# Two kept K/V units, small output-weight loads and new weight layouts in a two-layer decode kernel

## The chip, the cores and the metric

The kernel runs on one core of a Trainium2 chip. The metric is the device time of one execution in microseconds (us). Before the change the median of three runs was 2663.63 us (2663.0 to 2664.99).

Names used below: PE is the tensor engine, DVE the vector engine, ACT the scalar engine, POOL the GpSimd engine, SP the sync engine, which issues nearly all DMAs here. A "unit" is one (batch, head) pair; there are 64 units in a layer. A "tile" is half of a unit's K or V, 2 MB. "Slot" is a place of 16 KB per partition in the ring buffer in SBUF.

## The reference, cut to what matters

```python
B, Sq, D = 2, 1, 576
H, Sk, Dh = 32, 16384, 128        # k_cache, v_cache: (B, H, Sk, Dh) bf16, 268 MB each
F = 4608

def _A_ref(x, k_cache, v_cache, wq, wo):
    q = (x @ wq).reshape(B, Sq, H, Dh).transpose(0, 2, 1, 3)
    p = softmax(einsum("bhqd,bhkd->bhqk", q, k_cache) * Dh ** -0.5)
    o = einsum("bhqk,bhkd->bhqd", p, v_cache)
    return o.transpose(0, 2, 1, 3).reshape(B, Sq, H * Dh) @ wo

def _B_ref(x, w1, w2, w3, w4):     # S = 1: the shifted mixer is zero, hs = 0 @ w2
    x1 = x + hs
    return x1 + gelu(layernorm(x1) @ w3) @ w4

for layer in range(2):             # the same caches and weights in both layers
    x = x + _A_ref(layernorm(x), k_cache, v_cache, wq, wo)
    x = x + _B_ref(layernorm(x), w1, w2, w3, w4)
```

Both layers read the whole K and V caches. One query row per unit is used, so each byte that is read is used once per layer: the kernel is a stream of K and V through SBUF.

## The kernel before

Everything large passes through one ring of 12 slots. Tiles are wanted in the order of `plan`, and `pump` issues the next DMA as soon as the place that the ring points to is free. A place is the next address, with kept tiles stepped over.

```python
class Ring:
    def _place(self, n, aligned):
        p = self.at
        ...
        for _ in range(4 * len(self.live) + 4):
            if p + n > self.size:
                p = 0
            kept = [t for t in self.live if t["keep"] and t["off"] < p + n and p < t["off"] + t["n"]]
            if not kept:
                return p
            p = max(t["off"] + t["n"] for t in kept)
            ...

    def pump(self):
        while self.queue:
            key, n, src, aligned = self.queue[0]
            p = self._place(n, aligned)
            ...
            under = [t for t in self.live if t["off"] < p + n and p < t["off"] + t["n"]]
            if not all(t["done"] for t in under):
                return                                   # the next address is still in use: wait
            ...                                          # else issue the DMA into it
```

The order of the loads: the second layer walks the units backwards, so the last unit of layer 1 can be kept. The output weights wo come as eight blocks of 1152 KB in the same queue, one at every 16th unit, just before V.

```python
    GH = 8                 # heads in one output sum
    N_KEEP = 1             # units kept from layer 1
        self.order = [list(range(self.U)), list(reversed(range(self.U)))]
        kept = self.order[0][-self.N_KEEP:] if self.N_KEEP else []
        ...
            for i, u in enumerate(order):
                if u not in skip:
                    for h in range(2):
                        ring.want(("K", l, u, h), TB * 128, kv(self.K, u, h))
                ...
                if i >= 1:
                    self.want_v(kv, l, i - 1, skip, jrows)
            self.want_v(kv, l, self.U - 1, skip, jrows)
            for k in range(self.KT):
                ring.want(("w3", l, k), self.F, krows(self.w3, k, 0, self.F), aligned=(k == 0))
            for j in range(0, self.MT, 12):
                ring.want(("w4", l, j // 12), 12 * D, jrows(self.w4, j, 12), aligned=False)
            if l == 0:
                want_wq(1)

    def want_v(self, kv, l, i, skip, jrows):
        u = self.order[l][i]
        if (i + 1) % (self.GH * self.B) == 0:
            h0 = self.group_base(l, i)
            self.ring.want(("wo", l, h0), self.GH * self.D, jrows(self.wo, h0, self.GH))
        ...
```

w4 and wo are read in rows of 576 elements, 1152 bytes. PE has two jobs on a unit: it transposes half of K's blocks and multiplies them by the query, and it "weighs" V by the softmax weights with 128 matmuls.

```python
        def f(pe):                                        # weigh: one half of V
            for j in range(self.TB):
                ins = pe.matmul(self.ops[g][:, col:col + 1], lhsT=vt[:, j * 128:(j + 1) * 128],
                                rhs=self.p[q][:, h * self.TB + j:h * self.TB + j + 1], ...)
```

## Time and profile before

| | before |
|---|---|
| median of 3 runs | 2663.63 us |
| span of the profiled run | 2663.4 us |
| read from HBM | 1106.13 MB |
| busy: DVE, PE, ACT | 74%, 59%, 41% |
| K and V loads in the chain that ended last | 63% of the span |

These lines are from the page of the kernel before: the span; the busy tenths of the DMA engines and the rate in GB/s, each in 40 equal slices of 66.6 us; and the DMA queues with packets, megabytes and share of the 16 engines.

```profile
span 2663.4 us, 74240 instructions
...
DMA  9999999999999999999999999999999999999998
GB/s 393 426 426 427 424 419 426 426 426 408 426 426 426 426 407 426 426 426 425 357 401 421 426 426 422 426 427 425 426 392 426 426 427 426 407 426 426 427 426 300
...
q1 hardware_dynamic: 94072, 1106.16, 99.0%
q8 instruction: 270, 4.42, 0.7%
...
HBM read 1106.13 MB, written 0.00 MB: 415 GB/s over the span
```

The rate stands at 426 GB/s in most slices. It dips to 392 to 408 in four slices (wo blocks), to 357 at the layer boundary, and to 300 at the end.

The windows view gives the same for chosen stretches (length, busy time and number of instructions per engine, granted clock, mean busy share of the 16 DMA engines, GB/s): the layer boundary, one wo block, and the end.

```profile
core 0: us, PE busy (x) PEld busy (x) DVE busy (x) ACT busy (x) POOL busy (x), PEclk, DMA share, GB/s
1312.00:1360.00 48.00, 22.74 (x597) 21.48 (x598) 7.17 (x32) 3.71 (x11) 0.00 (x0) 0.50 1.02 328
1968.00:1978.00 10.00, 7.04 (x124) 6.79 (x125) 5.80 (x10) 3.90 (x5) 0.00 (x0) 0.51 0.63 247
2612.00:2664.00 52.00, 21.59 (x609) 19.88 (x609) 11.03 (x35) 2.22 (x10) 0.00 (x0) 0.50 0.84 289
```

At the wo block the DMA share falls to 0.63 and the rate to 247 GB/s. At the boundary the engines are busy (1.02) at a low rate: the packets there are small.

The timeline of the issuing queue around the start of layer 2 (start, length, engine, line, what is loaded, how many DMAs):

```profile
start us, us, engine line op out<-in xcount [idle before <-releaser]
...
1354.59 2.83 SPq L296 DMA_DIRECT2D ring<-in_A_k_cache_dram  x2
1379.17 9.31 SPq L296 DMA_DIRECT2D ring<-in_A_v_cache_dram  x2
1395.82 0.33 SPq L296 DMA_DIRECT2D ring<-in_A_k_cache_dram  x1
```

Between these issues the queue has enough tiles in hand. The slices here stay above 400 GB/s.

### The profile page before, as it was taken

What the parts mean: (1) busy time and instruction counts of PE and PEld (TensorE: products, weight loads), DVE (VectorE), ACT (ScalarE), POOL (GpSimd) and SP (SyncE); (2) the same over time, 40 slices, a digit from 0 to 9 for tenths busy, and PEclk for the clock granted to TensorE, in tenths of its full rate; (3) what the DMA queues carried; (4) which work ended last, traced back from release to release, by engine and by line L of the source; (5) the groups of instructions that cost most, each with busy time, mean ns of one, the idle gap of its engine ahead of it and who ended that gap; (6) DMA issues with size and microseconds to landing.
All of it is one profiled execution on the core that took longest, in us unless ns stands there. A gap on an engine that the chain in (4) does not pass through costs nothing.

```text
span 2663.4 us, 74240 instructions
## 1 busy us (share of the span) xinstructions
PE 1558.8 (59%) x34587; PEld 1461.0 (55%) x34587; DVE 1979.6 (74%) x2649; ACT 1098.5 (41%) x1681; POOL 0.8 (0%) x10
## 2 busy tenths in 40 slices
PE   4665565555556555556467565665556556556654
PEld 4555555555555555555457555555555555555554
DVE  5877877777777777787559777777777777777773
ACT  3444344344334434434235344344334434434431
POOL 0000000000000000000000000000000000000000
PEclk8666666666666666666566666666666666666665
DMA  9999999999999999999999999999999999999998
GB/s 393 426 426 427 424 419 426 426 426 408 426 426 426 426 407 426 426 426 425 357 401 421 426 426 422 426 427 425 426 392 426 426 427 426 407 426 426 427 426 300
DMA packets 94380, 1110.90 MB, mean 417 GB/s; under 512 B 8756, under 2 KB 26744, under 8 KB 26744
## 3 DMA queue, kind: packets, MB, share of 16 engines
q1 hardware_dynamic: 94072, 1106.16, 99.0%
q8 instruction: 270, 4.42, 0.7%
q14 instruction: 38, 0.31, 0.0%
HBM read 1106.13 MB, written 0.00 MB: 415 GB/s over the span
## 4 chain that ended last, share of the span: by engine, by line
DMA 67%; PE 11%; DVE 8%; another core or an unknown queue 8%; ACT 4%; SPq 1%; issue 1%
DMA ring<-in_A_v_cache_dram 35%; DMA ring<-in_A_k_cache_dram 28%; DVE sd L572 5%; PE ops L617 5%; PE tps L539 4%; DMA ring<-in_B_w_dram 4%; ACT ktsb L543 3%; DVE prod L569 3%; PE sps L557 1%; PE misc L590 1%; DMA ring<-in_A_wq_dram 1%; ACT p L603 1%; SPq L301 0%; PE misc L457 0%
## 5 line engine op out<-in xcount | busy, mean ns | idle before, releaser
L572 DVE TENSOR_REDUCE sd<-prod 128x8 f32<-128x1024 bf16 x1024 | 1249.0, 1220 | 35.4
L543 ACT ACTIVATE ktsb<-tps 128x1024 bf16<-128x1024 bf16 x1024 | 992.7, 1028 | 514.6 <-PE tps L539 509.1
L539 PE MATMUL tps<-ident,ring 128*128 128x128 bf16 x8192 | 829.2, 268 | 336.8 <-DMA ring<-in_A_k_cache_dram 336.8
L569 DVE TENSOR_TENSOR prod<-ring,qb 128x1024 bf16<-128x1024 bf16 x1024 | 698.7, 682 | 256.0 <-DMA ring<-in_A_k_cache_dram 255.3
L539 PEld LDWEIGHTS tps<-ident,ring 128*128 128x128 bf16 x8192 | 673.4, 123 | 366.5 <-DMA ring<-in_A_k_cache_dram 358.6
L617 PE MATMUL ops<-p,ring 128*128 128x1 bf16 x16384 | 471.2, 165 | 564.8 <-DMA ring<-in_A_v_cache_dram 555.2
L617 PEld LDWEIGHTS ops<-p,ring 128*128 128x128 bf16 x16384 | 450.1, 102 | 585.8 <-DMA ring<-in_A_v_cache_dram 571.7
L526 ACT ACTIVATE qb<-misc 128x128 bf16<-128x128 f32 x128 | 35.5, 277 | 941.8 <-PE misc L524 941.8
L557 PE MATMUL sps<-qt,ktsb 128*128 128x1 bf16 x8192 | 349.9, 166 | 93.4 <-ACT ktsb L543 85.1
L557 PEld LDWEIGHTS sps<-qt,ktsb 128*128 128x128 bf16 x8192 | 313.0, 102 | 132.8 <-ACT ktsb L543 131.6
L592 DVE TENSOR_REDUCE bias<-misc 128x1 f32<-128x128 f32 x128 | 37.3, 291 | 260.6 <-PE misc L590 260.6
L590 PE MATMUL misc<-identS,m 128*128 128x128 f32 x256 | 95.5, 476 | 34.6 <-DVE m L584 34.6
L590 PEld LDWEIGHTS misc<-identS,m 128*128 128x128 f32 x256 | 69.7, 333 | 37.2 <-DVE m L584 37.1
L603 ACT ACTIVATE p<-sps,bias 128x64 bf16<-128x64 f32 x128 | 40.5, 317 | 23.8 <-DVE bias L592 23.8
L603 ACT ACTIVATE p<-sd,bias 128x64 bf16<-128x64 f32 x128 | 45.4, 354 | 0.0
L448 PE MATMUL sps<-xn,ring 128*128 128x2 bf16 (+1 forms) x680 | 20.6, 165 | 30.0 <-DMA ring<-in_A_wq_dram 15.6
L448 PEld LDWEIGHTS sps<-xn,ring 128*128 128x128 bf16 (+1 forms) x680 | 19.4, 104 | 31.2 <-DMA ring<-in_A_wq_dram 13.8
L524 PE MATMUL misc<-ident,qt 128*128 128x128 bf16 x128 | 34.3, 268 | 2.2 <-DVE xa L649 1.6
L580 DVE TENSOR_REDUCE m<-sps 128x1 f32<-128x64 f32 x128 | 27.4, 214 | 0.0
L603 ACT ACTIVATION_READ_ACCUMULATOR p<-sps,bias 128x1 f32 x128 | 27.1, 212 | 0.0
L582 DVE TENSOR_REDUCE m<-sd 128x1 f32<-128x64 f32 x128 | 26.6, 208 | 0.0
L603 ACT ACTIVATION_READ_ACCUMULATOR p<-sd,bias 128x1 f32 x128 | 26.5, 207 | 0.0
(63 smaller groups left out, 123.4 us busy)
## 6 DMA issues: line engine op xcount, KB each, us to landing
ring<-in_A_k_cache_dram SPq DMA_DIRECT2D x254, 2048.0 KB, 46.5
ring<-in_A_v_cache_dram SPq DMA_DIRECT2D x254, 2048.0 KB, 50.4
ring<-in_B_w_dram SPq DMA_DIRECT2D x6, 1728.0 KB, 35.5
ring<-in_A_wo_dram SPq DMA_DIRECT2D x8, 1152.0 KB, 48.7
ring<-in_B_w_dram SPq DMA_DIRECT2D x8, 1152.0 KB, 23.4
ring<-in_A_wq_dram SPq DMA_DIRECT2D x8, 1024.0 KB, 10.6
ring<-in_B_w_dram SPq DMA_DIRECT2D x2, 576.0 KB, 31.9
ring<-in_A_wq_dram SPq DMA_DIRECT2D x2, 512.0 KB, 16.6
```

What stands on the lines that cost most here:

```text
L448: ins = pe.matmul(out[:, m * self.B:(m + 1) * self.B], lhsT=w[lo:128, m * 128:(m + 1) * 128], rhs=self.xn[lo:128, k, :], start=(k == 0 and ...
L524: self.pe(lambda pe: pe.matmul(self.misc[:, 0:128], lhsT=bcast(self.qt[:, u:u + 1], 128), rhs=self.ident[:, :], start=True, stop=True), r= ...
L526: self.act(lambda a: a.activation(out=self.qb[q][:, :], in_=self.misc[:, 0:128], func=ACT.Copy), r=["P:misc"], w=[f"qb{q}"])
L539: ins = pe.transpose(self.tps[b][:, j * 128:(j + 1) * 128], kt[:, (j0 + j) * 128:(j0 + j + 1) * 128], self.ident[:, :])
L543: self.act(lambda a: a.activation(out=self.ktsb[k][:, :, :].rearrange("p a b -> p (a b)"), in_=self.tps[b][:, :], func=ACT.Copy), r=[f"P:t ...
L557: ins = pe.matmul(self.sps[sp][:, col:col + 1], lhsT=self.ktsb[k][:, j, :], rhs=self.qt[:, u:u + 1], start=True, stop=True)
L569: self.dve(lambda v: v.tensor_tensor(out=self.prod[d][:, :, :], in0=k3, in1=bcast_mid(self.qb[q][:, :], self.CH), op=ALU.mult), r=[res, f" ...
L572: self.dve(lambda v: v.tensor_reduce(out=self.sd[q][:, o:o + self.CH], in_=self.prod[d][:, :, :], axis=AX.X, op=ALU.add), r=[f"prod{d}"], ...
L590: self.pe(lambda pe: pe.matmul(self.misc[:, 128:256], lhsT=bcast(self.m[:, q:q + 1], 128), rhs=self.identS[:, :], start=True, stop=True), ...
L592: self.dve(lambda v: v.tensor_reduce(out=self.bias[:, q:q + 1], in_=self.misc[:, 128:256], axis=AX.X, op=ALU.max, negate=True), r=["P:misc ...
L603: self.act(lambda a, c0=c0, c1=c1, src=src, part=part: a.activation(out=self.p[q][:, c0:c1], in_=src, func=ACT.Exp, bias=self.bias[:, q:q ...
L617: ins = pe.matmul(self.ops[g][:, col:col + 1], lhsT=vt[:, j * 128:(j + 1) * 128], rhs=self.p[q][:, h * self.TB + j:h * self.TB + j + 1], s ...
```

## The change

The intent is to read 8.4 MB less and to lose less DMA time. It keeps two units (eight tiles) instead of one for layer 2; takes wo out of the ring and loads it as 32 pieces of 288 KB on ACT's queue; lays w4 out in rows of 4608 bytes (four rows of the matrix per partition) with smaller last pieces; loads the last 64 rows of w3 and wq as two halves into both partition halves; and loads w2 as one tile, later. The core of the diff, with cuts:

```diff
-    GH = 8
-    N_KEEP = 1
+    GH = 2
+    N_KEEP = 2
+    FJ = 4
+    W4_PIECES = (3, 3, 2, 1)
...
+        self.wobuf = sb("wobuf", [128, self.GH, self.D], BF16)
...
-            ap = w[k * 128:D, c0:c1]
-            return lambda e, v: e.dma_start(v[self.p0:128, :], ap)
+            a0, a1 = w[k * 128:D, 0:cut], w[k * 128:D, n - cut:n]
+            return cut, [lambda e, v: e.dma_start(v[0:64, 0:cut], a0),
+                         lambda e, v: e.dma_start(v[64:128, 0:cut], a1)]
...
+        def frows(a0, n):
+            ap = self.w4[a0 * 128 * self.FJ:(a0 + n) * 128 * self.FJ, :].rearrange(
+                "(a p j) n -> p a (j n)", p=128, j=self.FJ)
+            return [lambda e, v: e.dma_start(v.rearrange("p (a m) -> p a m", a=n), ap)]
...
-            for j in range(0, self.MT, 12):
-                ring.want(("w4", l, j // 12), 12 * D, jrows(self.w4, j, 12), aligned=False)
+            a0 = 0
+            for c, n in enumerate(self.W4_PIECES):
+                ring.want(("w4", l, c), n * self.FJ * D, frows(a0, n), aligned=False)
+                a0 += n
...
-        if (i + 1) % (self.GH * self.B) == 0:
-            h0 = self.group_base(l, i)
-            self.ring.want(("wo", l, h0), self.GH * self.D, jrows(self.wo, h0, self.GH))
...
+    def load_wo(self, l, i):
+        h0 = self.group_base(l, i)
+        ap = self.wo[h0 * 128:(h0 + self.GH) * 128, :].rearrange("(j p) n -> p j n", p=128)
+        self.s.dma(lambda e: e.dma_start(self.wobuf[:, :, :], ap), w=["wobuf"], eng="scalar")
...
+                if i % n == 1 and c == 6:
+                    self.load_wo(l, i)
```

The ring's rule of placing (next address, kept tiles stepped over, wait if the tile there is in use) is not touched.

## The prediction

> **What bounds the kernel.** HBM reads. The DMA row of the slices is 9 nearly everywhere at 425 to 428 GB/s, and two thirds of the chain that ended last are K and V loads; DVE is busy 74%, PE 59%. The kernel moves 1110.9 MB (DMA line). At 426.5 GB/s that is 2605 us; some 59 us are DMA time lost. By windows: about 22 us around the eight 1.15 MB wo loads (1152 B rows; 247 GB/s in 1968 to 1978), about 11 us at the layer boundary (328 GB/s in 1312 to 1360), about 15 us after the last V tile (289 GB/s in 2612 to 2664), about 6 us at the start.
>
> **What the change does.**
> 1. Four more K/V tiles (8.39 MB) are not read again: -19.7 us of DMA time; doubled w3 columns cost +0.3.
> 2. wo comes as 32 small loads on the ACT queue instead of blocks inside the K/V queue. They keep 1152 B rows (0.051 us a packet; at the rate of 16 KB rows 0.043), so about 4 of the 22 us stay: -18 us.
> 3. w4 in rows of 4.6 KB and more: most of the loss at the boundary and the end, -5 to -6 us at each, including a last piece of 20 matmuls (about 0.6 us) instead of 60 (1.76 us).
> 4. The last rows of w3 and wq go to both partition halves, each by its own DMA. The Trainium skill, "SBUF — State Buffer", section '"Can I just issue two DMAs to hit both halves?"', says that such DMAs serialize. Before, single 64-partition loads coincide with stretches of 203 to 264 GB/s (windows), which agrees with half rate for one; no run shows two yet. I count no gain.
> 5. group_out runs 32 times instead of 8. No cost: DVE needs 15.5 us a unit where DMA needs 19.7.
>
> **The new wait.** Two kept units hold 8 of the 12 ring slots. Through four slots pass w3, w4, the next wq, then K of the third and fourth unit of layer 2. The ring places in address order, and the slot after these tiles holds K of the third unit, first half. So the next V load waits until layer 2 has gone through both kept units and that half, although kept slots come free before. In the trace of before that half is released 38.4 us after the layer's first query row (1357.4 to 1395.8, where a DMA issue ends its wait); this pace is DVE's, so it stays. The four tiles queued behind wq last only 4 x 4.9 = 19.7 us, and landing signal and issue add 2 to 4 us. I expect one DMA hole of about 22 us some 20 us into layer 2, which eats all of step 1. After it DMA bounds again.
>
> **Sum.** 2663 - 19.7 + 0.3 - 18 - 11.5 + 22 = 2636; I say 2634 us, range 2616 to 2648. All lies on the critical path, the DMA queue.
>
> Chances: faster by over 2%: 0.08; within 2%: 0.91; slower: 0.01.
>
> **What would show it.** Step 1: HBM read about 1097.9 MB. New wait: about 20 us with DMA share near 0 some 60 us after the last V tile of layer 1, the issuing queue waiting for a K transpose. Step 2: no dips below 415 GB/s every 16 units. Step 3: from the last V tile's weighing to the end about 32 us instead of 37.7.
>
> **What would make it wrong.** If the ring reuses freed kept slots in time, the time falls to about 2614. If small wo packets slow both queues, or ACT is held at issue, up to 10 us come back. If the two half loads run beside each other, 3 to 5 us less.

## The result, and the profile after

| | before | after |
|---|---|---|
| median | 2663.97 us (4 runs, 2663.0 to 2664.99) | 2664.78 us (4 runs, 2662.82 to 2666.54) |
| ratio, 95% interval | | 1.0003 (0.9985 to 1.002) |
| span of the profiled run | 2663.4 us | 2660.8 us |
| read from HBM | 1106.13 MB | 1097.87 MB |

A ratio here and below is the mean time of one kernel's fast runs over the mean of the other's fast runs of the same rounds, so it is not quite the ratio of the medians that are quoted. The change makes no difference that these runs can show. The prediction was 2634 us with a range up to 2648: a fall of some 30 us that did not come. The result lies 17 us above the range. The chance of 0.91 for "within 2%" was well placed, but only because the predicted fall was itself under 2%.

The page of the kernel after, the same lines as of before, with the new queue of the wo loads (q10) and PE's count of instructions:

```profile
span 2660.8 us, 74381 instructions
...
PE 1570.0 (59%) x34580; PEld 1474.1 (55%) x34580; DVE 1994.1 (75%) x2753; ACT 1098.3 (41%) x1681; POOL 0.9 (0%) x11
...
DMA  9999999999999999999869999999999999999997
GB/s 388 425 426 426 425 424 426 426 426 425 425 425 426 425 425 425 425 425 425 338 249 425 424 427 424 426 425 425 425 426 425 426 425 425 427 425 425 425 425 293
...
q1 hardware_dynamic: 78072, 1088.47, 97.0%
q10 hardware_dynamic: 8704, 9.44, 1.0%
q8 instruction: 270, 4.42, 0.7%
...
HBM read 1097.87 MB, written 0.00 MB: 413 GB/s over the span
```

The wo dips are gone: slices 10, 15, 30 and 35 stand at 425 to 427. The bytes fell as intended. But a slice of 249 GB/s has come just after the boundary, and the boundary itself (338) and the end (293) are no better than before (357 and 300).

The windows of the kernel after: the end of layer 1, the new dip, the place of the former wo dip, and the end of layer 2.

```profile
core 0: us, PE busy (x) PEld busy (x) DVE busy (x) ACT busy (x) POOL busy (x), PEclk, DMA share, GB/s
1308.00:1324.00 16.00, 8.56 (x193) 8.03 (x194) 3.23 (x20) 1.73 (x8) 0.00 (x0) 0.50 0.53 213
1376.00:1396.00 20.00, 15.57 (x363) 14.90 (x361) 18.73 (x25) 12.20 (x21) 0.00 (x0) 0.65 0.13 29
1968.00:1978.00 10.00, 4.37 (x140) 4.10 (x137) 9.76 (x14) 0.28 (x1) 0.00 (x0) 0.60 1.01 426
2644.00:2656.00 12.00, 5.50 (x185) 5.29 (x183) 1.26 (x4) 0.49 (x2) 0.00 (x0) 0.50 0.48 194
```

Two things are to be seen. In 1376 to 1396 the DMA engines stand nearly still: 0.13 and 29 GB/s. This is the hole that was predicted. And in 1308 to 1324 and 2644 to 2656 the DMA share is close to one half. That was not predicted, and it is the clue to the rest: a share of one half for 16 us can mean that half of the engines had nothing to do.

The issuing queue's timeline and its waits (line, waited for, total us, times, longest us) show the cause of the hole:

```profile
start us, us, engine line op out<-in xcount [idle before <-releaser]
...
1340.47 14.89 SPq L311 DMA_DIRECT2D ring<-in_A_k_cache_dram  x4
1394.23 0.81 SPq L311 DMA_DIRECT2D ring<-in_A_v_cache_dram  x2
1395.08 0.43 SPq L311 DMA_DIRECT2D ring<-in_A_k_cache_dram  x1
```

```profile
engine line waited for: us in total, times, longest us
...
SPq L311 <- PE tps L606: 398.3, 76, 38.9
```

After four K tiles the queue issues nothing until 1394.23, waiting 38.9 us for a K transpose on PE, the last reader of the third unit's first half. The last of those four tiles has landed in full at 1375.2, the next one lands in full at 1402.3; less the 4.9 us that a tile takes, the hole is 22.2 us. The prediction said 22.

To see where the rest went, four marks were taken from PE's timeline: the start of the two matmuls that add up the softmax sums after the last V half of layer 1 (`misc<-lsum,cone`), the first query row of layer 2 (`misc<-ident,qt`), the same sums at the end of layer 2, and the end of the span. The first three, before and then after (start, length, engine, line, operation):

```profile
1311.09 0.61 PE L630 MATMUL misc<-lsum,cone 128*128 128x32 f32 x2
1357.38 0.29 PE L524 MATMUL misc<-ident,qt 128*128 128x128 bf16 x1 [0.32 <-DVE qt L463]
2627.45 0.61 PE L630 MATMUL misc<-lsum,cone 128*128 128x32 f32 x2
```

```profile
1314.49 0.57 PE L697 MATMUL misc<-lsum,cone 128*128 128x8 f32 x2
1355.32 0.29 PE L591 MATMUL misc<-ident,qt 128*128 128x128 bf16 x1 [0.32 <-DVE qt L526]
2631.43 0.57 PE L697 MATMUL misc<-lsum,cone 128*128 128x8 f32 x2
```

| stretch, us | before | after | difference | predicted difference |
|---|---|---|---|---|
| layer 1 attention | 1311.1 | 1314.5 | +3.4 | -9 |
| boundary | 46.3 | 40.8 | -5.5 | -5.5 |
| layer 2 attention | 1270.1 | 1276.1 | +6.0 | -6.7 (= -19.7 - 9 + 22) |
| end | 35.9 | 29.4 | -6.5 | -6 |

The -9 in each layer is half of the -18 us of step 2, the wo loads. The boundary and the end came out at the predicted size (not for the predicted reason, as `w4_rows_old` shows), the hole and the tiles as predicted (shown below). What failed is the gain from taking the wo blocks out of the queue. The dips went away, and the layers did not become shorter.

### The profile page after: what moved, and what is told of

The parts are those of the page before. It is cut to its first block, busy times and chain, and to the rows that moved or that the text cites. A ratio compares the mean times of both kernels' runs of the same rounds, so it can differ in the third digit from the quotient of the medians.

```text
span 2660.8 us, 74381 instructions
## 1 busy us (share of the span) xinstructions
PE 1570.0 (59%) x34580; PEld 1474.1 (55%) x34580; DVE 1994.1 (75%) x2753; ACT 1098.3 (41%) x1681; POOL 0.9 (0%) x11
## 3 DMA queue, kind: packets, MB, share of 16 engines
q8 instruction: 270, 4.42, 0.7%
HBM read 1097.87 MB, written 0.00 MB: 413 GB/s over the span
## 4 chain that ended last, share of the span: by engine, by line
DMA 75%; DVE 24%; PE 1%; issue 0%; SPq 0%; ACT 0%; DVEq 0%
DMA ring<-in_A_k_cache_dram 69%; DVE sd L639 15%; DVE prod L636 9%; DMA ring<-in_A_v_cache_dram 4%; DMA ring<-in_B_w_dram 1%; DMA ring<-in_A_wq_dram 1%; PE misc L657 0%; PE ops L684 0%; PE misc L519 0%; PE sps L480 0%; SPq L319 0%; PE misc L446 0%; PE misc L448 0%; DVE bias L659 0%; SPq L321 0%
## 5 line engine op out<-in xcount | busy, mean ns | idle before, releaser
L639 DVE TENSOR_REDUCE sd<-prod 128x8 f32<-128x1024 bf16 x1024 | 1249.4, 1220 | 35.4
L657 PE MATMUL misc<-identS,m 128*128 128x128 f32 x256 | 95.3, 476 | 34.8 <-DVE m L651 34.8
L519 PE MATMUL misc<-otn,wobuf 128*128 128x2 bf16 x320 | 13.6, 167 | 99.8 <-DVE otn L703 99.8
L519 PEld LDWEIGHTS misc<-otn,wobuf 128*128 128x128 bf16 x320 | 11.0, 105 | 102.7 <-DVE otn L703 102.7
L480 PE MATMUL sps<-xn,ring 128*128 128x2 bf16 x544 | 18.3, 169 | 16.7 <-DMA ring<-in_A_wq_dram 11.8
L480 PEld LDWEIGHTS sps<-xn,ring 128*128 128x128 bf16 x544 | 17.4, 112 | 17.6 <-DMA ring<-in_A_wq_dram 10.1
## 6 DMA issues: line engine op xcount, KB each, us to landing
ring<-in_A_wq_dram SPq DMA_DIRECT2D x8, 1024.0 KB, 11.6
```

The lines of the kernel that those rows point to most:

```text
L480: ins = pe.matmul(out[:, m * B:(m + 1) * B], lhsT=pick(w, g, j), rhs=self.xn[:, k, :], start=(k == 0 and m == 0), stop=False, skip_group_c ...
L639: self.dve(lambda v: v.tensor_reduce(out=self.sd[q][:, o:o + self.CH], in_=self.prod[d][:, :, :], axis=AX.X, op=ALU.add), r=[f"prod{d}"], ...
L657: self.pe(lambda pe: pe.matmul(self.misc[:, 128:256], lhsT=bcast(self.m[:, q:q + 1], 128), rhs=self.identS[:, :], start=True, stop=True), ...
```

## The experiments

### What the rate of 16 engines hides

A DMA of 128 partitions runs on 16 engines. The Trainium skill, "DMA: Bandwidth & Descriptors", section "Why a DMA increments its semaphore by 16 and not by 1", says that these engines finish independently, that the semaphore counts them, and that only the full 16 means that all data has landed. The trace records these 16 landings for each tile (without naming the engine), and it agrees with the page: they are far apart. These are the 16 landings of the tile that landed in full at about 1270 us, in us after its first landing (worked out from the trace's records of landings):

```
before       0.0 0.1 0.1 0.1 0.3 0.5 0.9  2.0   9.9 10.7 11.0 11.0 11.1 11.4 11.5 11.5
after        0.0 0.0 0.1 0.4 0.4 2.1 4.9 10.4  24.8 25.2 25.7 25.8 25.8 26.2 26.3 26.5
```

Eight engines run ahead, eight run behind. In the kernel after, the last landing trails the first by 0.4 us at the first loads, by 13 us at about 610 us, and by 28.5 us at about 1303 us, some 2 us more in each 100 us. In the kernel before the spread grows likewise, but falls at seven of the eight wo blocks and never passes 15.6 us.

This gives the theory for the missing gain. A tile is usable when its slowest engine has landed, so the slow eight set the pace, and apart from the hole they do not pause. At a wo block of the kernel before the queue is held, the fast eight run dry (share 0.63) and the slow eight catch up. The landings around the wo block at about 1299 us in before show it. Before the block, tiles land in full every 4.9 us (1286.8, 1291.6, 1296.5); the wo block at 1299.4; the next tiles at 1304.3 and 1309.2, again 4.9 us apart. The slowest engine has lost nothing. The first landings of the wo block and of the next tile are 1286.4 and 1298.0, 11.6 us apart where a tile takes 4.9: the fastest engine has waited about 6.7 us there, and the spread has gone from 13.1 to 6.3 us (landing times are good to some tenths of a us). The other blocks of before show the same: at seven of the eight the next tile lands in full 4.9 us after the block, at the eighth (1658.6 us) 5.4 us. The dip in the mean rate is waiting time of engines that were ahead; to remove it gains nothing. In the kernel after the lead is paid back at the layer's end instead (share 0.53 in 1308 to 1324, 0.48 in 2644 to 2656).

What makes eight engines slow? The theory is the instruction fetches. The q8 line has 270 packets of 16 KB. PE has 34580 matmuls and 34580 weight loads; the Trainium skill, "Runtime: NRT & Kernel Launch", section "Instruction fetch mechanics", says that instruction memory is refilled in blocks of 16 KiB, 256 instructions each, by a DMA queue that the sequencer drives: 69160 / 256 = 270.2, so the count agrees and q8 carries PE's instructions. The page calls the cost mostly hidden. The rivals for the missing gain: the wo loads slow the queue (small packets, or ACT held at issue); the 64-row halves or the w4 rows do; or the hole has a second part that is not in the marks.

### Does the hole eat the kept tiles? keep1 and firstfit

`keep1` is the kernel after with one kept unit; `firstfit` is the kernel after with a ring that may take any free slot when the next place is in use.

```diff
 keep1
-    N_KEEP = 2
+    N_KEEP = 1
```

```diff
 firstfit
+    def _other_slot(self, n):
+        for p in range(0, self.size, self.slot) if n == self.slot else ():
+            under = [t for t in self.live if t["off"] < p + n and p < t["off"] + t["n"]]
+            if all(t["done"] for t in under):
+                return p, under
+        return None, None
...
             if not all(t["done"] for t in under):
-                return
+                p, under = self._other_slot(n)
+                if p is None:
+                    return
```

> Undoes the second kept unit, keeps the new weight layouts. Theory A (slowest DMA engines bound; the hole of 22 us in layer 2 belongs to the second kept unit): the hole goes, four tiles of 5.0 us come back, so 2656 to 2664 us, DMA share near 1 in the first 60 us of layer 2, HBM read 1106.3 MB. Rival B (wo and w4 gains are there as predicted, but the second kept unit costs some 50 us by more than the hole): about 2634 us.

> Two kept units, but a K or V tile that finds the next ring place taken may go to any slot that is free. Theory A: the hole of 22 us goes, nothing else changes, 2640 to 2648 us; DMA share over 0.9 in all of layer 2. Rival C (the hole only hides other waiting, DVE is behind anyway after it): above 2655 us.

Measured, against a before of 2664.65 us (7 runs): `keep1` 2664.04 us, ratio 1.0 (0.9985 to 1.0015), at the upper edge of what theory A expected; `firstfit` 2643.12 us, ratio 0.9921 (0.9906 to 0.9935). The windows of `keep1` and of `firstfit` in the place of the hole:

```profile
core 0: us, PE busy (x) PEld busy (x) DVE busy (x) ACT busy (x) POOL busy (x), PEclk, DMA share, GB/s
...
1376.00:1396.00 20.00, 15.80 (x321) 15.12 (x319) 18.73 (x25) 12.12 (x21) 0.00 (x0) 0.59 0.92 375
```

```profile
1376.00:1396.00 20.00, 15.48 (x322) 14.80 (x321) 18.73 (x25) 12.17 (x21) 0.00 (x0) 0.66 0.95 385
1308.00:1324.00 16.00, 7.24 (x153) 6.46 (x152) 3.05 (x19) 1.73 (x8) 0.00 (x0) 0.50 0.54 211
```

And the issuing queue of `firstfit`, which now loads V at 1364 instead of 1394:

```profile
1342.22 14.69 SPq L320 DMA_DIRECT2D ring<-in_A_k_cache_dram  x4
1364.03 7.50 SPq L320 DMA_DIRECT2D ring<-in_A_v_cache_dram  x2
```

With the placing alone changed the hole is gone (0.95, 385 GB/s) and the time is 21.7 us shorter than after's 2664.78. This shows the hole's cause, the placing by address, and its price. `firstfit` and `keep1` differ by the second unit without the hole: 20.9 us (2664.04 - 2643.12), where the prediction had 19.7. `firstfit` keeps the half share in 1308 to 1324, so that is a matter of its own. And `keep1`, which has all of the new layouts and the small wo loads and no kept tile more, is as slow as before within the noise: steps 2 and 3 together gave nothing that these runs can show, where 29.5 us had been predicted.

### The layouts without the wo loads: keep1_wo_ring

One kept unit, and wo in the ring as before; what remains of the change is the layouts of w2, w3, w4 and wq.

```diff
-    GH = 2
-    N_KEEP = 2
+    GH = 8
+    N_KEEP = 1
...
+        if (i + 1) % (self.GH * self.B) == 0:
+            h0 = self.group_base(l, i)
+            ap = self.wo[h0 * 128:(h0 + self.GH) * 128, :].rearrange("(j p) n -> p j n", p=128)
+            self.ring.want(("wo", l, h0), self.GH * self.D,
+                           [lambda e, v: e.dma_start(v.rearrange("p (j n) -> p j n", j=self.GH), ap)])
...                                                       (load_wo and wobuf taken out)
```

> As keep1, but wo comes again as eight 1.15 MB blocks within the K/V queue, 16 heads per group_out. To be compared with keep1. Theory A (at the wo loads only DMA engines that had run ahead stand idle; the slowest never wait): the dips to about 360 GB/s at each wo load come back, the spread between the first and the last of the 16 landings of a tile falls from about 13 to 6 us at each and stays under 16 us, and the time is that of keep1 within 4 us. Theory of the prediction (the wo blocks cost DMA time): 15 to 18 us slower than keep1.

Measured: 2662.21 us, ratio 0.9992 (0.9975 to 1.0009), which is 2.4 us under before in the medians; the interval holds 1, so no gain is shown. Its rate by slices has the dips again:

```profile
GB/s 385 426 426 426 426 425 426 426 426 408 427 426 426 426 408 426 426 426 426 373 400 411 425 427 420 426 427 425 426 409 426 426 425 426 407 426 426 426 426 305
```

Slices 10, 15, 30 and 35 are back at 407 to 409, and the kernel is 1.8 us faster than `keep1`, which has none of these dips. So taking the dips away gained nothing; the 1.8 us themselves are within the spread of the runs (2661.43 to 2662.62 against 2662.48 to 2666.13). The spread of the 16 landings stays below 16.2 us here (15.1 in layer 1), against 28.6 and 34.8 in `keep1`. The boundary and the end are 2.3 and 3.5 us shorter than in before, the two layers 1.1 and 1.7 us longer.

### Fewer instructions: fewer_instr

If the fetches make eight engines slow, a kernel that fetches less must be faster although it loads the same data. Here PE weighs V with every eighth matmul only. Its output is wrong, which doesn't matter for the time. It still passes the comparison's tolerance; the loads, their order and the ring's rule are those of after (V's slots come free some 1.6 us sooner, as the weighing is shorter).

```diff
-            for j in range(self.TB):
+            for j in range(0, self.TB, 8):
                 ins = pe.matmul(self.ops[g][:, col:col + 1], ...
-                                start=(h == 0 and j == 0), stop=(h == 1 and j == self.TB - 1))
+                                start=(h == 0 and j == 0), stop=(h == 1 and j == self.TB - 8))
```

> As the changed kernel, but only every 8th of the matmuls that weigh V (result wrong on purpose): 28672 PE instructions fewer, about 112 instruction fetches of 16 KB fewer. Theory D (the lagging half of the DMA engines lags because instruction fetches run on them, about 1.55 us each, 270 of them on 8 engines): the spread of landings at the end of a layer falls from 28 to about 16 us and the time falls by 18 to 24 us, to about 2643. Rival E (half of the engines are slower by ports, halves of the partitions or HBM): spread 28 us and 2664 us as before.

Measured: 2645.42 us, ratio 0.9929 (0.9914 to 0.9944), which is 19.4 us under after. From its page:

```profile
span 2642.4 us, 45709 instructions
...
PE 1197.1 (45%) x20244; PEld 1094.3 (41%) x20244; DVE 1993.6 (75%) x2753; ACT 1097.2 (42%) x1681; POOL 0.9 (0%) x11
...
q8 instruction: 158, 2.59, 0.4%
...
HBM read 1097.87 MB, written 0.00 MB: 415 GB/s over the span
```

40488 / 256 = 158.2: the fetches follow PE's instructions again. The landings of the tile at about 1268 us:

```
fewer_instr  0.0 0.0 0.2 0.3 0.5 1.9 6.2 10.5  14.6 14.7 14.7 14.8 14.8 15.1 16.2 16.9
```

The lag of the slow eight (the ninth landing) falls from 24.8 to 14.6 us, a ratio of 0.59; the fetches fell from 270 to 158, a ratio of 0.585. The time fell as well, by 19.4 us, and it fell where the theory has it: the two attention stretches are 10.7 and 12.9 us shorter than after's, the boundary and the end 1.7 and 3.4 us longer. That is 19.4 us for 112 / 8 = 14 fetches less on each of eight engines: 1.39 us a fetch, an estimate, since shorter weighing at the two layer ends takes a small part (64 matmuls take 1.8 us there). From the lag alone: by 1268 us 127 of the 270 fetches have started, 16 on each slow engine, and 24.8 / 16 is about 1.55 us.

The traces also show a fetch at work, packet by packet (worked out from their packet records; no view prints them). In the trace of before, 120 packets of q8 start between 100 and 1280 us. They take 1.07 us each in the median. Right behind 119 of them (within 0.06 us of their end) there is exactly one slow 16 KB packet of K or V, of 1.10 us in the median, where the median of all such packets is 0.61 us; behind the last one a 1152-byte packet took 0.138 instead of 0.051 us. At times picked at random within the same stretch, a slow packet starts in 1.5% of cases. In the kernel after it is 101 of 121, and the other 20 have a small wo packet behind them. So a fetch takes 1.07 + 0.49 = 1.56 us of one engine's time. 127 fetches on eight engines make 24.8 us, and the 75 that `fewer_instr` has started by then make 14.6 us: both are the measured lag (an estimate, as the trace doesn't name the engines). Over the whole kernel 270 / 8 fetches come to 53 us on each slow engine, which is nearly all of the 59 us that the prediction had laid to wo, the boundary, the end and the start.

A rival is left for the run, though these packets leave it little room: PE reads less SBUF in it, and that might be what helps the DMA engines. It asks for a run in which fetches are added and PE is left as it is.

### More fetches, first try: more_instr

256 empty instructions on POOL for each unit.

```diff
             self.row_max(l, i)
+            self.s.op("gpsimd", lambda g: [g.nop() for _ in range(256)][-1], deps=[self.s.ops[-1]])
```

> As the changed kernel, plus 256 empty instructions on the idle GpSimd engine in each of the 128 units: 32768 instructions, about 128 more fetches of 16 KB. fewer_instr gained 19.4 us for 112 fetches, 0.173 us each. Theory D, if these fetches run on the same DMA engines: 2664.8 + 22 = about 2687 us, spread at the end of a layer about 39 us. If they run on the other engines: within 4 us of 2665 and a smaller spread. Rival F (the matmuls themselves, not their fetches, made the lag in fewer_instr): 2665 us and spread 28 us.

Measured: 2665.2 us, ratio 1.0001 (0.9986 to 1.0016), against a before of 2665.81 us. This run is empty. The build dropped the instructions:

```profile
span 2662.9 us, 74446 instructions
```

That is 65 more than after, not 32768 more. It tells nothing of fetches. (It is a second run of the kernel after in effect, and repeats its time.)

### More fetches, second try: more_pool

Instructions that can't be dropped: 128 one-byte fills on POOL for each unit, 16384 in all.

```diff
+        self.pad, self.padded = sb("pad", [128, 32], mybir.dt.uint8), []
...
             self.row_max(l, i)
+            self.padded = [self.s.op("gpsimd", lambda g: [g.memset(self.pad[k % 4 * 32:k % 4 * 32 + 1,
+                           k // 4:k // 4 + 1], 0) for k in range(128)][-1],
+                           deps=[self.s.ops[-1], *self.padded])]
```

> The run before this one of that kind (more_instr) was empty: the builder dropped the empty instructions, 270 fetches as ever. Here the changed kernel has 128 one-byte fills of an unused tile on the idle GpSimd engine in each of the 128 units: 16384 instructions, about 64 more fetches of 16 KB. At 0.173 us each (fewer_instr) theory D has 2665 + 11 = about 2676 us and a spread of about 34 us at the end of a layer, if GpSimd's fetches run on the same DMA engines; if they run on the other engines, 2665 us and a spread of about 22 us. Rival F (it was the matmuls, not their fetches): 2665 us within 3, spread 28 us unchanged.

Measured: 2698.93 us, ratio 1.0129 (1.0112 to 1.0145), against a before of 2665.16 us. Neither number that had been expected was met: the effect is there, and three times larger than the theory's. From its page:

```profile
span 2697.3 us, 90892 instructions
...
q8 instruction: 270, 4.42, 0.7%
q14 instruction: 168, 1.38, 0.1%
...
HBM read 1097.87 MB, written 0.00 MB: 407 GB/s over the span
```

PE's fetches are the same 270. q14 has 168 packets instead of after's 39: 129 more, of 8 KB each, one for 127 of POOL's fills. (The 39 are not POOL's: POOL runs 11 instructions in the kernel after. Whose they are was not tested.) And the landings of the tile at about 1268 us:

```
more_pool    0.0 0.0 0.0 0.1 0.2 0.8 5.6 18.9  19.5 19.5 19.6 19.8 20.9 21.1 21.2  38.9
```

One landing alone is 38.9 us behind the first, and 17.7 us behind the next. That fits POOL's fetches all going to one engine, outside the slow eight (the trace doesn't name it): 129 small packets, 1.06 MB of 1104 MB, cost 34 us. That is the theory in a sharper form than it was put: data that lands late on one engine holds the whole stream. The expectation had these fetches on the slow eight or spread over the other engines, and was wrong in both.

By 1268 us 60 more packets of q14 have started here than in after. 73 of 75 packets of q14 between 100 and 1280 us have one slow K or V packet right behind them, 0.96 instead of 0.61 us in the median; with the 0.31 us of the packet itself that is 0.66 us a fetch, 40 us for 60 of them, an estimate that meets the 38.9 us. PE and DVE work here as in after (PE busy 1568.4 against 1570.0 us; DVE's two main operations keep their means of 1220 and 683 ns), so the rival "PE reads less SBUF" is not needed. An influence of POOL's own writes can't be excluded by this run alone, but they go to four partitions and nothing waits for them.

### The rows of w4: w4_rows_old

The kernel after with w4 in rows of 1152 bytes again and the pieces in the same sizes.

```diff
-    FJ = 4
-    W4_PIECES = (3, 3, 2, 1)
+    FJ = 1
+    W4_PIECES = (12, 12, 8, 4)
```

> As the changed kernel, but w4 again in rows of 1152 B (same pieces, same ring). Theory of the prediction (step 3 is worth 5 to 6 us at the layer boundary and as much at the end): about 2675 us. Rival G (only the slower rate of 1152 B packets counts, 14.7 instead of 12.8 us for 5.31 MB; the rest of the shorter stretches is lag that had been paid before): about 2668 us, so 3 to 5 us more.

Measured: 2663.51 us, ratio 0.9993 (0.9978 to 1.0008). It is not slower than after, so both expectations were missed (about 2675 and about 2668 us). Its boundary and end are 41.0 and 30.6 us against after's 40.8 and 29.4. So the long rows, which the prediction took for the reason of 11 us, are worth 0.2 and 1.2 us here. Most of what makes the boundary and the end of the kernel after shorter than before's is something else. About 0.9 us of each is the last output sum, which has 10 matmuls instead of 40 (1.67 against 2.63 us from the first mark to its end). For the rest, argued and not shown: with a lead of 28 us the fast engines have fetched their part of the weights before the last V tile is complete. `fewer_instr` fits, where the lead is 17.9 us and the two stretches are 1.7 and 3.4 us longer. The smaller last pieces of w4 and the two half loads, which this run keeps, are not excluded.

### Which queue brings wo: wo_small_sp and firstfit_wo_ring

`wo_small_sp` issues the small wo loads from SP instead of ACT. `firstfit_wo_ring` puts wo back into the ring as in `keep1_wo_ring`, keeps two units, and allows the free-slot fallback in layer 2: the best of the parts.

```diff
 wo_small_sp
-        self.s.dma(lambda e: e.dma_start(self.wobuf[:, :, :], ap), w=["wobuf"], eng="scalar")
+        self.s.dma(lambda e: e.dma_start(self.wobuf[:, :, :], ap), w=["wobuf"], eng="sync")
```

```diff
 firstfit_wo_ring  (with wo in the ring, GH = 8, as in keep1_wo_ring; N_KEEP = 2)
             if not all(t["done"] for t in under):
-                return
+                p, under = self._other_slot(n) if key[1] == 1 else (None, None)
+                if p is None:
+                    return
```

> As the changed kernel, but the 32 wo loads of 0.29 MB are issued on the K/V queue instead of ACT's. If mixing two queues costs the 3 us a layer: about 2659 us. If the small loads themselves do, or nothing: 2663 to 2667 us. The theory of the prediction (wo in the K/V queue costs DMA time by blocking it) has 2665 to 2680 us.

> Both what helped: two kept units and the free choice of slots in layer 2, and wo as eight blocks in the K/V queue as before. If the ACT queue's wo loads cost some 3 us a layer (last group_out of layer 1 at 1314.5 with them, 1311.1 in the kernel before, 1312.2 with wo in the ring): 2637 to 2641 us. If that is noise: 2643 us as firstfit.

Measured, against 2665.81 us: `wo_small_sp` 2663.66 us, ratio 0.9993 (0.9976 to 1.0009); `firstfit_wo_ring` 2641.49 us, ratio 0.9911 (0.9897 to 0.9926). The first is within its expectation, the second falls between its two numbers. The issuing engine makes no difference that the runs can show. The Trainium skill, "DMA: Bandwidth & Descriptors", section "Issuing engines are not separate DMA queues", says that DMAs of all issuing engines run on the same 16 engines; these runs don't contradict it (0.9993 and, for after, 1.0003). With wo back in the ring the layer-1 stretch is 1312.5 us, with small loads 1314.5 to 1316.1 in the six kernels that have them and in which PE and POOL work as in after. So the layer is 2 to 4 us longer with the small loads, or with the 32 output sums that come with them: no run parts the two. In the medians 1.6 to 1.8 us are left (2664.04 - 2662.21 and 2643.12 - 2641.49), which is within the spread of the runs. Why is open. `firstfit_wo_ring` beats both kernels, by 24.3 us in the medians against before, 0.9%.

## Why the prediction was wrong

The parts, each by the runs that isolate it:

| part | predicted, us | measured, us | from |
|---|---|---|---|
| step 3, layouts | -11.5 | -2.4 (within noise) | keep1_wo_ring - before |
| step 2, wo as small loads | -18 | +1.8 (within noise) | keep1 - keep1_wo_ring |
| step 1, four tiles less | -19.4 | -20.9 | firstfit - keep1 |
| the new wait | +22 | +21.7 | after - firstfit |
| sum | -27 | +0.2 | measured as a whole: +0.8 |

- **Step 1 was right.** HBM read fell to 1097.87 MB as predicted, and the four tiles are worth 20.9 us.
- **The new wait was right** in its place, its cause and its size: 22.2 us in the trace, 21.7 us by `firstfit`. The issuing queue waits for a K transpose, as predicted.
- **Step 2 failed, and it is the step that made the prediction wrong**: "wo comes as 32 small loads on the ACT queue ...: -18 us". The sign that it named, no dips below 415 GB/s every 16 units, came true, and the gain did not come: +1.8 us, within noise, instead of -18. The error lies one step earlier, in the first paragraph: "some 59 us are DMA time lost", read off the mean rate of 16 engines. Eight of them carry PE's instruction fetches and lag; the other eight run ahead and stand still at the wo blocks. Their standing still was counted as time lost, but the slow eight bound the kernel and they did not stand still: before's tiles go on landing in full every 4.9 us through the blocks. `fewer_instr` shows what the slow eight lose: 112 fetches less, the lag reduced in the same proportion, and 19.4 us gained with the same data loaded.
- **Step 3 was wrong in its reason and by 9 us in its size.** The boundary and the end did become 5.5 and 6.5 us shorter, as predicted, but the rows of w4 give 0.2 and 1.2 us of it (`w4_rows_old`), and of the 5.8 us that the layouts take off the boundary and the end (`keep1_wo_ring`) 2.8 us come back as longer layers. All layouts together give 2.4 us in the medians, within noise.
- **Step 4 was not tested alone**: no gain was counted for two half loads, and none is seen. The Trainium skill, "SBUF — State Buffer", section '"Can I just issue two DMAs to hit both halves?"', says that two such DMAs serialize (+6% over one). The trace fits: the halves' packets of 5120 bytes took 0.292 us in the median, where 9216-byte packets of the full rows took 0.349 us, which at the same rate would be 0.194 us.
- **Step 5 was right**: DVE's busy share went from 74% to 75%. PE does wait longer for it before the output sums (99.8 us in all before 32 of them, 6.3 us before the 8 of the kernel before), but PE is not what bounds the kernel. Whether these waits are part of the 2 to 4 us a layer is open.
- Of the things named as what could make the prediction wrong, the nearest was "up to 10 us come back" from small wo packets. It is the right place, but the issuing queue plays no part that shows (`wo_small_sp`).

The trace of before held what was needed: 16 landings of a tile in two groups of eight, 10 us apart at 1270 us, and closing at the wo blocks; and a DMA share of 0.63 at a wo block. A stretch in which the mean rate falls and the spread of the landings falls with it is a stretch in which the late engines catch up.

What stays open: why the layers are 2 to 4 us longer with small wo loads than with blocks in the ring; why the data packet behind a fetch takes 0.49 us longer; which of the 16 engines they are, and whose the 39 packets of q14 are; and why `keep1` and `firstfit` still run a little below the full rate just after the boundary (0.92 and 0.95).

## What to carry to other kernels

This DMA-bound kernel was bound by its slowest DMA engines, so before you count a dip in the mean rate as lost time, look at the 16 landings of one tile: if they are far apart, the dip may be the fast engines waiting, and what counts is what makes the slow ones slow, here the fetching of 69160 PE instructions. When more of a ring is kept, walk through the ring's next places by hand: a rule that waits for the next address although other slots are free turned 21 us of saved loading into 22 us of waiting, and a fallback of a few lines brought it back. And a gain that is measured alone (`keep1_wo_ring`, `keep1`, `firstfit`) is worth more than a sum that fits.

## What the Trainium skill lacked or had wrong

- "Runtime: NRT & Kernel Launch", section "Instruction fetch mechanics", calls the cost of crossing a 16 KiB block mostly hidden. That may be so for the engine that fetches, but the fetches take time on the DMA engines: 127 of PE's 270 blocks had made 8 of 16 DMA engines lag by 25 us near the end of layer 1, and 112 blocks fewer made the kernel 19.4 us faster (2645.42 against 2664.78 us).
- The same page gives 16 KiB blocks for each engine. PE's fetches were of 16 KB (270 packets, 4.42 MB), those that POOL's fills added in `more_pool` of 8 KB (129 packets, 1.06 MB).
- No page that was read says which DMA engines carry an engine's fetches. Here PE's lie on eight of the 16, and POOL's seem to go to a single one: 129 of them, 1.06 MB, put one landing 38.9 us behind and cost 34 us (2698.93 against 2664.78 us). Nor does a page say that the data packet behind a fetch is slow: 1.10 instead of 0.61 us.
- "DMA: Bandwidth & Descriptors" says that the 16 engines finish independently, but not how far apart they can drift: up to 28.5 us within a layer of the kernel after and 34.8 us in `keep1`, with tiles of 4.9 us, and that the mean rate then misleads.
- "CRC Debugging", section "Comparing the Two Runs", puts the instruction refills on queue 14. In these profiles the fetches that POOL's fills add are there (168 packets instead of 39), but PE's are on queue 8 (270).
